# Attention with a routed feed-forward block: a builder's clock that lets loads overlap, and earlier ranks for V tiles 8 to 15

## The chip, the cores and the metric

The kernel runs on one core of one Trainium2 chip. The metric is the device time of one execution in microseconds (us). The core's engines are TensorE (PE, with its weight loads shown apart as PEld), VectorE (DVE), ScalarE (ACT) and GpSimd (POOL); SyncE (SP) issues nearly all DMAs.

## The reference

```python
B, S, D = 8, 3136, 256;  d_qk = 64;  F = 1024;  cap = 128
scores = (z @ z.T) / S                       # per batch, S x S, symmetric
attn = np.maximum(scores, 0.0) ** 2
x = u * (attn @ v)                           # S x D
s = x @ w_gate                               # per batch: one score per row
top = the 128 rows with the largest s
out = x;  out[top] = x[top] + sigmoid(s[top]) * (relu(x[top] @ w1) @ w2)
```

Everything is float32. Nearly all of the work is `z @ z.T` and `attn @ v` for 8 batches of 3136 rows; the routed part touches 128 rows per batch.

## The kernel before, in words

**Tiles.** A batch's 3136 rows are cut into six chunks of 512 queries and a remainder of 64 (`CHUNKS`), and into 24 tiles of 128 keys and a half tile of 64. Two neighbouring key tiles make a pair; a slot is one chunk of queries against one pair of key tiles. A slot's squared scores times V are added up in PSUM (`acc`, one for each half of the 256 columns, in two rotating accumulators), with V as the weights and the squares as the moving data, so the result stands transposed.

**Splitting.** PE multiplies rounded float32 (`F32R`). To keep the precision every operand is split in a rounded part and its remainder: `ZH` and `ZL`, the two halves of a `V` tile, and `hi` and `lo` of a slot's squares. A slot takes 16 matmuls with `hi` (both parts of V) and 8 with `lo` (rounded V alone), each over half of the rows of PE. A rounded part is made by ACT (a CAST or an ACTIVATE); a remainder is one subtraction of two operands in SBUF, on POOL or DVE, whichever the builder expects to end first. `lent` is a `hi` and `lo` pair that stands in a tile of the ring that otherwise holds `qk`.

**Symmetry.** The squares are symmetric, so a chunk computes only blocks with keys from its own chunk on. New blocks are made on PE (`sc`), lifted by ACT (`a`), squared, split, and also transposed on DVE (`aT`) and stored to DRAM (`squares`, `squares_own` for half of the diagonal block, `squares_last` for the remainder's keys). Later chunks fetch them as `qk`, `own` and `rest`; `rest_hl` holds both parts of a remainder block. A batch ends with its last chunk, made mostly of old blocks, with the 64 remainder rows among them, while the next batch's Z and V are already loaded and split; the next batch's first chunk is made of new blocks alone.

**V.** `stage_v` loads four V tiles (512 rows) with four DMAs into a tile `vst` of a ring of two, and `prep_v` rounds them pair by pair. The last use of a pair of the old batch frees its place for the new batch. In the first chunk of a batch the pairs are used in the order 0, 2 to 9, half tile, 10, 1, 11, and they are loaded and rounded in groups of two pairs in this order of first use.

**The order.** No order is written by hand. The Python builder keeps a clock for each engine and for the DMA queue (`Clock`, with constants for each kind of operation) and emits all engines' instructions in one program. Each waiting piece of work off PE is a job with a rank; among the jobs that can start, the one that starts first on that clock goes first, and the lower rank when they tie. PE is filled with whatever the clock says is ready. So the clock's times and the ranks set the order on every engine, and each engine then runs its own stream in that order on the chip. Ranks are counted in slots: a job of rank k belongs to slot k.

**What the change touches.** `Clock.move` (line 147) is the clock's account of a DMA: `begin` is when it may start, and `free(out)` is when earlier readers and writers of the part of the tile that it writes have ended. `free` has a second argument, `by`: entries of that engine are then left out. `prep_v` (line 759) sets the rank of the rounding of V and of its remainder, and the loop at lines 2653 to 2657 sets the rank of the loads of V; `k0` is the first slot of the batch and `first_use` the first slot that uses a pair. `fetch_rest` (line 860) issues two DMAs into one tile, whose columns alternate between the two.

Of the kernel before, what the change touches and what calls it, by code (L numbers as in the profile page):

```python
# [90 lines left out]
class Clock:  # L91
# [55 lines left out]
    def move(self, out, src, by):  # L147
        n = run = 1
        for _, c in out.ap:
            n *= c  # L150
        for s, c in sorted(src.ap, key=lambda x: x[0]):
            if s == run:
                run *= c
        short = 1
        for s, c in sorted(out.ap, key=lambda x: x[0]):
            if s == short:
                short *= c
        run = min(run, short, n)
        far, near = (x.space == bass.MemoryType.DRAM for x in (out, src))
        known = {(True, False): self.STORES.get(n), (False, True): self.LOADS.get(n), (False, False): self.INSIDE}.get((far, near))  # L160
        large = near and n > P * 2 * CH
        wait, took, more = known or (3.17 if large else 1.4, (1.25 if large else 1.0) * n / run * (0.008 + 0.000038 * 4 * run) / 16, 0.8)
        begin = max(self.at[by], self.after(src) + 0.06, 0.0 if far else self.free(out) + 0.06)
        self.at[by] = begin + (0.6 if far or out.ap[0][1] == 64 else 0.47 if out.ap[0][1] <= Q else 0.53)
        self.queue = max(self.queue, begin + wait, 2.4) + took
        return self.queue + more
# [179 lines left out]
def attention_then_routed_ffn(ctx: ExitStack, tc: tile.TileContext, zt, ut, v, wg, w1, w2, cst, cst16, keys, outs, at, cap):  # L346
# [43 lines left out]
    v_ring = Ring(stage, [P, GT, D], "vst", 2)  # L390
# [45 lines left out]
    def job(on, rank, fn, reads=(), rings=(), ok=None, took=None, locks=False):  # L436
        on = on.split("|")
        ready = reads if callable(reads) else max((clock.after(x) for x in reads), default=0.0) + 0.05
        j = Job(on, rank, fn, ready, rings, ok, took, locks)
        for e in on:  # L440
            pending[e].append(j)
# [81 lines left out]
    def more_steps(chain, steps):  # L523
        chain.steps.extend(steps)
        wake(chain)
# [6 lines left out]
    def round_on(e, hi, src):  # L532
        (nc.scalar.copy if e == "act" else ON[e].tensor_copy)(hi, src)

    def rest_on(e, lo, src, hi):
        ON[e].tensor_tensor(lo, src, hi.bitcast(F32), op=ALU.subtract)

    def takes(n):
        return {"pool": 0.15 + 0.00219 * n, "dve": 0.16 + 0.00104 * n + SPARE, "act": 0.19 + 0.00083 * n}
# [103 lines left out]
    for e in range(2):  # L643
        for f in range(0, NF // 2, 2):
            g = e * NF // 2 + f
# [25 lines left out]
    def stage_z(b, i, n=None, step=None, uses=1, queues=None):  # L671
        a, w = part(i)
        n = n or w
        if n > CH:
            st = old_ring.take("zall", uses=uses).rearrange("p f k -> p (f k)")
        else:
            st = z_ring.take("zst", uses=uses)
        for h in range(2):
            (queues or (nc.sync, nc.sync))[h].dma_start(st[h * 64 : h * 64 + 64, : step or n], zt[b, :, a : a + (step or n)])
        staged["z", b, i] = st  # L680

    def more_z(b, i, of):

        a, n = part(i)
        o = a - part(of)[0]
        for h in range(2):
            nc.sync.dma_start(staged["z", b, of][h * 64 : h * 64 + 64, o : o + n], zt[b, :, a : a + n])
# [49 lines left out]
    def z_free(b, i):  # L737
        return issued > max(last_key[b - 1, i], last_moving[b - 1, i])

    def stage_v(b, g, queues=None):  # L740

        whole = g < NJ // GT
        st = v_ring.take("vst", uses=2 if whole else 1)
        if whole:
            for f in range(GT):
                src = v[b, g * CH + f * P : g * CH + (f + 1) * P, :].rearrange("(t a) d -> a t d", a=Q)
                (queues or [nc.sync] * GT)[f].dma_start(st[f * Q : (f + 1) * Q], src)
        else:
            for h in range(2):
                nc.sync.dma_start(st[h * 64 : h * 64 + 64, 0, :], v[b, NJ * P :, :])  # L750
        staged["v", b, g] = st
        for i in range(2 if whole else 1):
            prep_v(b, 2 * g + i)
# [5 lines left out]
    def prep_v(b, g):  # L759

        st = staged["v", b, g // 2]
        src = st[:, g % 2 * 2 :]
        n = 2 if 2 * g < NJ else 1
        ring = pair_ring if n == 2 else half_ring
        src = src[:, :n].rearrange("p a d -> p (a d)").rearrange("p (f h i) -> p h f i", h=NK, i=Q)
        rank = first_use[b, g] + (-0.5 if b or g > 1 else 0.5)
        order = b * (NJ // 2 + 1) + sum((first_use[b, i // 2 * 2], i) < (first_use[b, g // 2 * 2], g) for i in range(NJ // 2 + 1))

        def high(e):
            t = ring.take("V", F32R)  # L770
            vtile[b, g] = t
            parts_of = [t[:, w].rearrange("p h (f i) -> p h f i", i=Q) for w in range(2)]
            round_on(e, parts_of[0], src)
            vnext[0] = order + 1
            for q in range(n):
                V[b, 2 * g + q] = t[:, :, :, q * P : (q + 1) * P]
            job("pool|dve", rank, lambda e: low(e, parts_of), [src, parts_of[0]], took=takes(n * D))

        def low(e, parts_of):
            rest_on(e, parts_of[1], src, parts_of[0])  # L780
            for q in range(n):
                vlow[b, 2 * g + q] = True
            v_ring.drop(st)

        landed = clock.after(src) + (SLACK if b else 0.05)
        turn = lambda: vnext[0] == order and (order < 2 or now[0] > 0 or 0 in parts)
        job("act" if b else "act|dve" if g > 1 else "dve", rank, high, lambda: landed, [ring], turn, takes(n * D), True)
# [31 lines left out]
    begins, ends, last_key, first_use, last_use, last_moving = {}, {}, {}, {}, {}, {}  # L819
# [551 lines left out]
    def load_u(b, c):  # L1371
        c0, w = CHUNKS[c]
        t = u_ring.take("ut")
        nc.sync.dma_start(t, ut[b, :, :, c0 : c0 + w].rearrange("h p t -> p h t"))
        chunk[b, c] = t
# [1256 lines left out]
    def at_slot(k, fn):  # L2632
        plan.setdefault(max(k, 0), []).append(fn)

    def load(k, rank, fn, rings=(), ok=None, reads=()):
        late = lambda: max([0.0] + [clock.after(x) for x in reads])
        at_slot(k, lambda: job("sp", rank, lambda e: fn(), late, rings, ok))

    for b in range(B):
        k0 = first_of[b, 0]  # L2640
        for c in range(NCH):
            if c < WHOLE:
                load(ends[b, c] - 9, ends[b, c] - 2, lambda b=b, c=c: load_u(b, c), (u_ring,))
        if b:

            def get_z(b=b, i=0):
                stage_z(b, i)
                prep_z(b, i, now[0] + 5)

            for i in range(NCH):  # L2650
                k = max(last_key[b - 1, i], last_moving[b - 1, i]) - LEAD + 1
                load(k, k0 - 12 + i, lambda b=b, i=i: get_z(b, i), (z_ring,), lambda b=b, i=i: z_free(b, i))
            for g in range(0, NJ // 2 + 1, 2):
                k = last_use[b - 1, g]
                before = [x for x in range(0, NJ // 2 + 1, 2) if first_use[b, x] < first_use[b, g]]
                ok = lambda k=k, b=b, before=before: now[0] >= k - 2 and all(("v", b, x // 2) in staged for x in before)
                load(max(k - 4, k0 - 16), k0 - 14 if g < 4 else first_use[b, g] - 4, lambda b=b, g=g: stage_v(b, g // 2), (v_ring,), ok)
        elif b == 0:
            load(0, 1, lambda: (more_z(0, 4, 1), prep_z(0, 4, 2, 1)))
            load(1, 2, lambda: (stage_z(0, FIFTH, S + 64 - FIFTH * CH, uses=2), prep_z(0, FIFTH, 4, FIFTH), prep_z(0, WHOLE, 5, FIFTH)), (old_ring,))  # L2660
            for g in range(4, NJ // 2 + 1, 2):
                k = first_use[0, g]
                load(max(0, k - 8), k - 4, lambda g=g: stage_v(0, g // 2), (v_ring,))
        at_slot(first_of[b, 2], lambda b=b: more_steps(far, turn_rest_u(b)))

    order_of = {}
    for k, (b, c, js, is_old) in enumerate(slots):
        key = b, c, js[0] // GT
        if is_old and c < WHOLE and key not in order_of:
            n = order_of[key] = len(order_of)  # L2670
            ok = lambda key=key, n=n: fetches[0] == n and stored.get((key[0], key[2], key[1])) == 2
# [6 lines left out]
        elif is_old and c == WHOLE:  # L2678
            g = js[0] // GT
            ok = lambda b=b, g=g: all(stored.get((b, g + i, WHOLE)) == 2 for i in range(2))  # L2680
# [37 lines left out]
    far = chain_of([], 3)  # L2718
# [171 lines left out]
```

## Time and profile before

| | us |
|---|---|
| median of 3 runs | 2033.03 (2032.85, 2033.03, 2036.61) |
| the profiled execution's own time | 2036.05 |
| its span, first to last instruction | 2034.2 |
| PE busy | 2000.0 (98%) |
| DVE, ACT, POOL busy | 1538.1, 1482.4, 1557.7 (76%, 73%, 77%) |
| DMA | 408.49 MB, mean 201 GB/s |

Busy time is counted from the records of instructions; PE runs two matmuls at a time, one on each half of its rows, and their ends are modelled, so the idle time between them is more telling than the busy share. The granted clock is 0.999 of full speed over the span. All program rows carry line 248, that of the recording helper, so rows are told apart by the names of their tiles. In the timeline a bracket at a row's end gives the time in which the engine stood idle before it, and what ended it.

### The profile page before, as it was taken

The numbers are of one execution on the slowest core, as the hardware profiler recorded it, in microseconds if no ns is written. First come the engines' busy times: TensorE is split into PE (matmuls) and PEld (weight loads), VectorE is DVE, ScalarE is ACT, GpSimd is POOL, SyncE is SP. The second block draws the span as 40 slices with busy tenths as digits, with TensorE's granted clock in tenths as the row PEclk, the third lists the DMA queues.
The fourth block names the chain that finished last, engine by engine and source line by source line (L and its number), as shares of the span: only waits on it lengthen the run. The fifth ranks groups of instructions, "written<-read, shape, count | busy, mean of one in ns | idle before, by whom it ended". The sixth has DMA issues, their size and how long they took to land. (4 is left out here: it accounts for less than half of the span.)

```text
span 2034.2 us, 45720 instructions
## 1 busy us (share of the span) xinstructions
PE 2000.0 (98%) x17226; PEld 1642.6 (81%) x17226; DVE 1538.1 (76%) x2563; ACT 1482.4 (73%) x1816; POOL 1557.7 (77%) x1096
## 2 busy tenths in 40 slices
PE   9999999999999999999999999999999999999998
PEld 6999878888787788888877788877887888877776
DVE  7776777667887758767789766887677676797786
ACT  8886788767887658776787657886678776887652
POOL 7787887779877778678977777867697777888662
PEclk9999999999999999999999999999999999999999
DMA  6899867886688767878767787778877868766862
GB/s 191 238 250 247 210 188 213 205 199 170 198 236 194 199 191 223 221 194 193 183 208 199 192 209 202 218 199 217 214 180 228 218 175 205 194 186 184 219 170 75
DMA packets 421614, 408.49 MB, mean 201 GB/s; under 512 B 128910, under 2 KB 329232, under 8 KB 421392
## 3 DMA queue, kind: packets, MB, share of 16 engines
q1 hardware_dynamic: 420224, 403.07, 74.3%
q8 instruction: 135, 2.21, 0.5%
q0 software_dynamic: 800, 2.10, 0.3%
q14 instruction: 87, 0.71, 0.1%
q10 hardware_dynamic: 368, 0.39, 0.1%
HBM read 230.08 MB, written 175.37 MB: 199 GB/s over the span
## 5 line engine op out<-in xcount | busy, mean ns | idle before, releaser
L248 PE MATMUL acc<-hi,V 64*128 64x512 f32 x8752 | 1153.9, 390 | 3.7 <-DVE sum L248 2.5
L248 PEld LDWEIGHTS acc<-hi,V 64*128 64x128 f32 x8752 | 844.0, 185 | 159.1 <-DVE sum L248 4.7
L248 PE MATMUL acc<-lo,V 64*128 64x512 f32 x4232 | 619.9, 391 | 9.9 <-POOL lo L248 6.3
L248 POOL TENSOR_TENSOR lo<-a,hi 128x512 fp32r<-128x512 f32 x288 | 450.4, 1572 | 183.3 <-ACT a L248 108.1
L248 POOL TENSOR_TENSOR lo<-qk,hi 128x512 fp32r<-128x512 f32 x315 | 486.9, 1561 | 72.1 <-ACT hi L248 45.3
L248 PEld LDWEIGHTS acc<-lo,V 64*128 64x128 f32 x4232 | 409.7, 184 | 95.3 <-POOL lo L248 17.8
L248 ACT ACTIVATE hi<-a 128x1024 fp32r<-128x1024 f32 (+2 forms) x385 | 346.8, 901 | 99.2 <-PE acc L248 66.0
L248 DVE STREAM_TRANSPOSE aT<-a 128x512 f32<-128x512 f32 (+2 forms) x622 | 383.5, 646 | 36.4 <-ACT a L248 25.2
L248 ACT ACTIVATE a<-a 128x1024 f32<-128x1024 f32 (+1 forms) x351 | 332.3, 949 | 78.2 <-DVE a L248 65.3
L248 ACT ACTIVATE a<-sc 128x1024 f32<-128x1024 f32 (+2 forms) x344 | 325.0, 945 | 76.7 <-PE sc L248 39.6
L248 DVE TENSOR_TENSOR lo<-a,hi 128x512 fp32r<-128x512 f32 x243 | 262.7, 1085 | 148.2 <-ACT a L248 75.9
L248 ACT CAST hi<-qk 128x1024 fp32r<-128x1024 f32 x240 | 249.4, 1046 | 138.9 <-PE acc L248 73.4
L248 DVE TENSOR_TENSOR lo<-qk,hi 128x512 fp32r<-128x512 f32 x165 | 180.3, 1105 | 55.1 <-ACT hi L248 49.9
L248 POOL TENSOR_TENSOR lo<-own,hi 128x256 fp32r<-128x256 f32 x94 | 100.7, 1091 | 82.5 <-ACT hi L248 55.0
L248 PE MATMUL sc<-ZH 64*128 64x512 f32 (+2 forms) x728 | 153.9, 381 | 5.9 <-ACT a L248 4.2
L248 PE MATMUL sc<-ZL,ZH 64*128 64x512 f32 (+2 forms) x728 | 152.2, 376 | 0.0
L248 PE MATMUL acc<-lent,V 64*128 64x512 f32 x1128 | 141.0, 390 | 3.8 <-POOL V L248 2.3
L248 POOL TENSOR_TENSOR ut<-x,w_run 128x512 f32<-128x512 f32 x90 | 131.5, 1474 | 9.1 <-DVE x L248 8.0
L248 PE MATMUL sc<-ZH,ZL 64*128 64x512 f32 (+2 forms) x680 | 132.2, 371 | 0.0
L248 PEld LDWEIGHTS acc<-lent,V 64*128 64x128 f32 x1128 | 105.2, 184 | 29.5 <-POOL V L248 4.0
L248 POOL TENSOR_TENSOR ut<-sum,ut 128x512 f32<-128x512 f32 x68 | 93.6, 1377 | 40.3 <-DVE sum L248 30.5
L248 POOL TENSOR_TENSOR lent<-a,lent 128x512 fp32r<-128x512 f32 x64 | 90.8, 1431 | 26.6 <-DVE a L248 14.1
(233 smaller groups left out, 1823.7 us busy)
## 6 DMA issues: line engine op xcount, KB each, us to landing
squares<-aT SPq DMA_DIRECT2D x240, 512.0 KB, 4.4
qk<-squares SPq DMA_DIRECT2D x480, 256.0 KB, 6.2
ut<-in_ut SPq DMA_DIRECT2D x48, 512.0 KB, 7.9
vst<-in_v SPq DMA_DIRECT2D x190, 128.0 KB, 3.2
out<-x SPq DMA_DIRECT2D x188, 128.0 KB, 4.2
squares_own<-aT SPq DMA_DIRECT2D x47, 256.0 KB, 2.0
own<-squares_own SPq DMA_DIRECT2D x188, 64.0 KB, 2.9
zst<-in_zt SPq DMA_DIRECT2D x85, 128.0 KB, 5.3
```

The lines of the kernel that those rows point to most:

```text
L248: got = real(*args, **kw)
```

## The change

The builder's clock no longer lets a DMA wait for earlier DMAs of the same queue into the same part of a tile, or out of it. From the second batch on, the rounding of V pairs 4 to 7 (tiles 8 to 15) and its remainder get a rank 4.5 slots ahead of their first use instead of 0.5, and these tiles are loaded with the rank of the first eight (14 slots ahead of the batch) instead of 4 slots ahead of their first use.

```diff
@@ Clock.move
-        begin = max(self.at[by], self.after(src) + 0.06, 0.0 if far else self.free(out) + 0.06)
+        begin = max(self.at[by], self.after(src) + 0.06, 0.0 if far else self.free(out, by) + 0.06)
@@ prep_v
-        rank = first_use[b, g] + (-0.5 if b or g > 1 else 0.5)
+        rank = first_use[b, g] - (4.5 if b and 4 <= g < 8 else 0.5 if b or g > 1 else -0.5)
@@ the loads of V, for b > 0
-                load(max(k - 4, k0 - 16), k0 - 14 if g < 4 else first_use[b, g] - 4, lambda b=b, g=g: stage_v(b, g // 2), (v_ring,), ok)
+                load(max(k - 4, k0 - 16), k0 - 14 if g < 8 else first_use[b, g] - 4, lambda b=b, g=g: stage_v(b, g // 2), (v_ring,), ok)
```

The three lines emit no instruction of their own; they change which piece of work the builder takes next. The kinds of instructions and their counts stay, but for the slots whose `hi` and `lo` stand in a lent tile (47 before, 44 now), and for remainders that go to POOL or to DVE. The order is the same on every engine up to some 245 us into the program and differs from there to nearly the end.

On PE, at the end of the first batch: `sc` rows are scores of the next batch, `hi`, `lo` products of the last old slots. Before:

```order
L248 MATMUL acc<-hi,V 128x512 x12
L248 MATMUL acc<-lo,V 128x512 x8
L248 MATMUL sc<-ZH 128x512 x2
L248 MATMUL sc<-ZH,ZL 128x512 x2
L248 MATMUL sc<-ZL,ZH 128x512 x2
L248 MATMUL acc<-hi,V 128x512 x14
L248 MATMUL acc<-lo,V 128x512 x2
L248 MATMUL acc<-hi,V 128x512 x2
L248 MATMUL acc<-lo,V 128x512 x2
L248 MATMUL acc<-hi,V 128x512 x8
L248 MATMUL acc<-lo,V 128x512 x6
```

The same place on PE now:

```order
L248 MATMUL acc<-hi,V 128x512 x16
L248 MATMUL acc<-lo,V 128x512 x8
L248 MATMUL acc<-hi,V 128x512 x8
L248 MATMUL sc<-ZH 128x512 x2
L248 MATMUL sc<-ZH,ZL 128x512 x2
L248 MATMUL sc<-ZL,ZH 128x512 x2
L248 MATMUL acc<-lo,V 128x512 x4
L248 MATMUL acc<-hi,V 128x512 x8
L248 MATMUL acc<-lo,V 128x512 x4
L248 MATMUL acc<-hi,V 128x512 x8
L248 MATMUL acc<-lo,V 128x512 x4
```

The last two old slots ran as 14, 2, 2, 2, 8 and 6 matmuls and now run as alternating groups of 8 `hi` and 4 `lo`. The old sequence stands at five of the seven batch ends, the new one at four, and a fifth is close to it.

On POOL, at the same place: `V` rows are remainders of V tiles of the next batch, `lo<-qk,hi` those of old slots, `ZL` and `ZH` those of the next batch's Z. Before:

```order
L248 TENSOR_TENSOR V<-vst,V 128x512 x2
L248 TENSOR_TENSOR lo<-qk,hi 128x512 x2
L248 TENSOR_TENSOR rest_hl<-rest,rest_hl 128x8x64
L248 TENSOR_TENSOR lent<-a,lent 128x512
L248 TENSOR_TENSOR ZL<-zst,ZH 128x4x4x32
L248 TENSOR_TENSOR lent<-a,lent 128x512
L248 TENSOR_TENSOR lo<-qk,hi 128x512 x3
L248 TENSOR_TENSOR V<-vst,V 128x512 x2
```

The same place on POOL now:

```order
L248 TENSOR_TENSOR V<-vst,V 128x512 x2
L248 TENSOR_TENSOR lo<-qk,hi 128x512 x2
L248 TENSOR_TENSOR ZL<-zst,ZH 128x128
L248 TENSOR_TENSOR ZH<-zst,ZH 128x64
L248 TENSOR_TENSOR lo<-qk,hi 128x512 x2
L248 TENSOR_TENSOR V<-vst,V 128x512 x2
L248 TENSOR_TENSOR lent<-a,lent 128x512
L248 TENSOR_TENSOR ut<-sum,ut 128x512
```

Between the first two V pairs and the next two POOL had five `lo<-qk` rows, three of them at the end, and two `lent`; now it has four `lo<-qk` and no `lent`.

On SP, from the first chunk of the second batch: `vst` rows are loads of V (four to a group of four tiles, `64x256` the half tile), the other loads and stores are as named above. Before:

```order
L248 DMA squares_own_0_120<-aT 128x512
L248 DMA zst<-in_zt 64x128 x2
L248 DMA out<-xr 64x256
L248 DMA vst<-in_v 32x4x256 x4
L248 DMA squares_0_97<-aT 512x1x256 x2
L248 DMA vst<-in_v 64x256 x2
L248 DMA squares_0_97<-aT 512x1x256
L248 DMA qk<-squares_0_97 32x4x512 x4
L248 DMA out<-x 32x16x64 x4
L248 DMA squares_0_97<-aT 512x1x256 x2
L248 DMA own<-squares_own_0_120 32x4x128 x4
L248 DMA vst<-in_v 32x4x256 x4
```

The same place on SP now:

```order
L248 DMA zst<-in_zt 64x128 x2
L248 DMA vst<-in_v 32x4x256 x12
L248 DMA squares_own_0_120<-aT 128x512
L248 DMA out<-xr 64x256
L248 DMA vst<-in_v 64x256 x2
L248 DMA squares_0_97<-aT 512x1x256 x3
L248 DMA qk<-squares_0_97 32x4x512 x4
L248 DMA out<-x 32x16x64 x4
L248 DMA squares_0_97<-aT 512x1x256
L248 DMA vst<-in_v 32x4x256 x4
L248 DMA squares_0_97<-aT 512x1x256
L248 DMA own<-squares_own_0_120 32x4x128 x4
```

Tiles 16 to 19 are now loaded in one row of twelve DMAs with tiles 8 to 15, ahead of the store of `squares_own`, and the last load of V (tiles 20 to 23) has moved ahead of the `own` fetch.

## Rows read from the trace of the kernel before

**Rows 1.** The page's first part: busy us (share) xinstructions.

```profile
PE 2000.0 (98%) x17226; PEld 1642.6 (81%) x17226; DVE 1538.1 (76%) x2563; ACT 1482.4 (73%) x1816; POOL 1557.7 (77%) x1096
```

**Rows 2.** Busy time by stretch: stretch, its us, busy us (xinstructions) by engine.

```profile
250.00:300.00 50.00, 47.90 (x411) 37.77 (x410) 39.52 (x58) 41.34 (x53) 42.52 (x31) 1.00 0.62 183
490.00:545.00 55.00, 51.82 (x446) 41.31 (x445) 44.81 (x85) 45.13 (x58) 47.34 (x35) 1.00 0.60 178
740.00:985.00 245.00, 244.98 (x2150) 203.16 (x2148) 183.19 (x230) 188.07 (x229) 190.22 (x132) 1.00 0.77 202
985.00:1040.00 55.00, 52.17 (x450) 41.39 (x448) 45.46 (x85) 45.51 (x58) 47.02 (x35) 1.00 0.60 179
1040.00:1120.00 80.00, 75.55 (x666) 61.15 (x664) 74.50 (x151) 60.57 (x69) 58.56 (x44) 1.00 0.72 201
...
1500.00:1545.00 45.00, 43.97 (x375) 34.53 (x373) 39.06 (x55) 37.39 (x49) 40.62 (x30) 1.00 0.64 184
1740.00:1800.00 60.00, 58.44 (x505) 46.03 (x503) 52.75 (x112) 51.40 (x64) 53.12 (x39) 1.00 0.54 162
1985.00:2034.20 49.20, 39.47 (x285) 31.56 (x281) 32.60 (x122) 10.69 (x23) 11.07 (x10) 1.00 0.20 67
```

**Rows 3.** PE's waits from 250 to 2000 us: total us, times, longest us.

```profile
PE acc L248 <- POOL lo L248: 6.3, 9, 1.0
PE sc L248 <- ACT a L248: 2.6, 2, 1.3
PE acc L248 <- POOL V L248: 2.3, 4, 0.9
PE acc L248 <- DVE lo L248: 2.0, 1, 2.0
PE acc L248 <- DVE sum L248: 1.9, 6, 0.5
```

**Rows 4.** PE in order of time: start us, us, row [idle before, releaser].

```profile
254.16 0.50 PE L248 MATMUL acc<-lo,V 64*128 64x512 f32 x2 [0.95 <-POOL lo L248]
...
292.24 0.74 PE L248 MATMUL acc<-lent,V 64*128 64x512 f32 x4 [0.90 <-POOL V L248]
...
1743.49 0.50 PE L248 MATMUL acc<-lo,V 64*128 64x512 f32 x2 [0.95 <-POOL lo L248]
```

**Rows 5.** DVE and POOL in order of time, at two routing steps.

```profile
597.24 0.90 DVE L248 TENSOR_TENSOR lo<-a,hi 128x512 fp32r<-128x512 f32 x1
...
1092.54 7.14 DVE L248 TENSOR_TENSOR lo<-a,hi 128x512 fp32r<-128x512 f32 x1
...
1091.56 2.62 POOL L248 TENSOR_TENSOR ut<-x,w_run 128x512 f32<-128x512 f32 x2
...
1096.61 2.52 POOL L248 TENSOR_TENSOR lo<-qk,hi 128x512 fp32r<-128x512 f32 x2
```

**Rows 6.** SP's DMA issues in order of time, 230 to 290 us.

```profile
232.94 1.18 SPq L248 DMA_DIRECT2D rest<-squares_last  x2
...
240.29 7.86 SPq L248 DMA_DIRECT2D vst<-in_v  x8
248.52 0.34 SPq L248 DMA_DIRECT2D squares_own<-aT  x1
...
280.41 2.88 SPq L248 DMA_DIRECT2D own<-squares_own  x4
283.46 1.74 SPq L248 DMA_DIRECT2D vst<-in_v  x4
```

**Rows 7.** POOL and ACT in order of time at the first boundary.

```profile
251.39 5.38 POOL L248 TENSOR_TENSOR lo<-qk,hi 128x512 fp32r<-128x512 f32 x3
...
256.81 1.06 ACT L248 ACTIVATE lent<-a 128x1024 fp32r<-128x1024 f32 x1 [3.00 <-POOL lo L248]
```

**Rows 8.** Groups of instructions by form: xcount | busy us, mean ns | idle before.

```profile
L248 POOL TENSOR_TENSOR V<-vst,V 128x512 fp32r<-128x512 f32 x63 | 89.5, 1428 | 2.7 <-ACT V L248 1.4 <-DVE V L248 1.0 <-DMA vst<-in_v 0.4
```

**Rows 9.** ACT in order of time, where PE waits for scores near 537 us.

```profile
536.76 1.02 ACT L248 ACTIVATE a<-sc 128x1024 f32<-128x1024 f32 x1 [2.12 <-POOL lo L248]
```

## The prediction

> **What bounds the kernel now.** I read the busy times first. The reader is to see that PE is busy 2000.0 of the 2034.2 us of the span [rows 1]. The change adds and removes no product, so PE's work stays and only its 34.2 us of idle time is in play. Second come the stretches of the span, to see where that idle time lies [rows 2]: span minus PE is 2.10, 3.18, 2.83, 1.03 and 1.56 us in the five stretches around 250, 490, 990, 1500 and 1745 us, 10.70 in all. These are five of the seven places where one batch ends and the next begins. The batch boundary near 745 us falls at the head of a stretch of 245 us in which PE is idle 0.02 us, so such a boundary can be crossed without a stop. The last 49.2 us have 9.73 us of idle time, and 1040 to 1120 us has 4.45. Third I asked what PE waits for behind 250 us [rows 3]: lower halves of attention squares from POOL (6.3 us in 9 waits), roundings of V from POOL (2.3 in 4), scores waiting for ACT's `a` (2.6 in 2), and sums that free an accumulator (1.9 in 6). Fourth, the order of time on PE puts them at the boundaries [rows 4]: at 254.16 us 0.95 for `lo`, at 292.24 us 0.90 for V, and at 1743.49 us again 0.95 for `lo`. The `lo` wait of about 0.95 us stands at four boundaries (254, 494, 990 and 1743 us; 3.8 us together).
>
> **The time that the sum starts from.** The profiled execution took 2036.05 us, 1.85 us around its span. The median of the other runs is 2033.03, and the three are 2032.85, 2033.03 and 2036.61: two levels some 3.3 us apart, and the profile is on the upper one. The trace shows what may part them: one DVE subtraction at 1092.54 us took 7.14 us, where the same step of the routing, two batches earlier, took 0.90 [rows 5], and PE waited 2.0 us for it [rows 3]. I take 3.0 us off for that (2036.05 to 2033.03) and predict an execution without it.
>
> **The builder's clock (line 163).** `fetch_rest` issues two DMAs into interleaved columns of one tile. The old clock starts the second only when the first has ended, by its own constants 2.7 us later; in the trace SP issues such a pair in 1.18 us [rows 6]. So the plan was too late about these tiles and is now nearer to what the queue does. The clock issues nothing, it only moves choices, and PE's order is unchanged to its row 390, some 245 us in. From there the first eight V DMAs of the next batch stand behind a `qk` load and a Z load instead of ahead of them, `rest_hl` is multiplied whole before `hi`, and the last old slots of the batch run as regular groups of `hi` 8 and `lo` 4. In the old order PE reaches `lo` two matmuls at a time, which is what a starved engine looks like in an order.
>
> **The `lo` wait.** Before, POOL does three `lo` from 251.39 to 256.77 us, in a row, and ACT stands 3.00 us behind them before it can write the next `lent` tile [rows 7]. In the old order the last two ACT casts that feed these halves stand back to back, after nine other ACT rows; in the new one the first of the two comes before that, with four rows between them, and POOL does the halves in pairs with V and Z work between. I expect all four waits to go: -3.8 us. Bounds: -3.8, or nothing if the new last pair is as late. The five sums behind them (about 1.5 of the 1.9 us) I leave standing, since ACT still copies the accumulator just after a `lent` write.
>
> **The V waits.** They are not for tiles 8 to 15 themselves but for tiles 20 to 23, loaded last: only two staging tiles exist, so what is rounded earlier frees staging earlier. Before, the four DMAs of the last load are issued at 283.46 us, behind an `own` fetch of 2.88 us [rows 6]. In the new order they stand ahead of that fetch and of one store, so some 2.9 us earlier if SP comes to this place at the same time, against a wait of 0.90 at most. All four go: -2.3 us; bounds -2.3 and 0.
>
> **What V displaces.** The new rank places four V remainders of a batch ahead of `lo` work of slots up to four later. One costs POOL 1.43 us [rows 8]; the work is the same, only earlier. The scores' wait near 537 us follows from such a crowding: ACT stood 2.12 us behind a POOL `lo` [rows 9], which had begun behind a V remainder. Two such waits, 2.6 us; still two late V remainders stand near there, so I take half: -1.3, bounds -2.6 and 0 (and more than 0 in a rival below).
>
> **Added waits on SP.** After the boundary SP's order now has twelve V DMAs in a row where it had eight. With two staging tiles the last four wait for a rounding, and behind them on SP stand the store of `squares_own`, one of `xr` and then stores of `squares`. In the old order the eight already took 7.86 us with their waits, the store went out at 248.52 and was first read at 280.41 us [rows 6], so 32 us hide a delay of some microseconds. Cost nothing; if that cover were gone, it would be half of such a block more, some 4 us, at each boundary.
>
> **What else moves.** From row 391 on everything shifts, also far from V. Three fewer of the first chunk's tiles are kept in a lent tile, and seven `rest_hl` and seven Z remainders go from POOL to DVE, whose count of two-input operations stays about the same (511 and now 515 in the orders). New stops elsewhere lie between 0 (the stretch with 0.02) and 4.45 (the worst stretch without a starved boundary) [rows 2]; a gain there is possible too, but 9.3 us of the idle time outside the named stretches lies mostly before 250 us, where nothing moves. I take +1.5, nearer to the long quiet stretch. The end, from the last batch's own remainder on, has the same sequence in both orders (106 rows on PE), so its 9.73 us stay.
>
> **Sum.** 2036.05 - 3.0 - 3.8 - 2.3 - 1.3 + 1.5 = 2027.1 us, that is 5.9 below the median shown.
>
> **Rivals.** (B) *The wait only changes its owner.* At the boundary the next chunk needs an accumulator as well, and ACT's copy comes after the `lent` write that itself waits for the last `lo`. For it: sum waits, up to 0.5 us, are there already [rows 3]. Against it: the boundary near 745 us shows neither. Then only the V waits go: 2033.03 - 2.3 = 2030.7.
> (C) *V ahead of `lo` starves PE.* The remainders of tiles 8 to 15, put 4.5 slots ahead, land on POOL before the `lo` that PE needs next. Price: one of 1.43 us at each of five boundaries, 7.2 us, with none of the gains: 2040.2, slower. It decides from 4.1/7.2, more than half a remainder per boundary before the last `lo`. For it: ACT's and PE's waits behind POOL today. Against it: in the new order two `lo` pairs stand ahead of the second V pair, where three `lo` stood behind two V.
> (D) *Collisions of POOL and DVE.* In the 7.14 us case POOL ran six operations from 1091.56 to 1099.13 us without a pause, and DVE ended right after them [rows 5]. If the new order meets this twice in every execution, 2 x 3.0 us eat the gain: 2027.1 + 6.0 = 2033.1. The Trainium skill says in "SBUF — State Buffer" (Who interferes with whom) that a DVE operation with two SBUF inputs and a GpSimd operation exclude each other for a whole instruction, and that whichever was issued first decides. By that rule alone a DVE step would lose one POOL operation, some 1.3 us, and the case would cost nothing that can be measured; the trace shows a loss over six in a row, so the rule bears out the collision but not its size.
>
> **How the numbers follow.** The runs of this kernel agree within some 0.2% (4.1 us), so less than that can't be told from no change: below 2029.0 is faster, above 2037.1 slower. My forecast has 0.56 (0.53 of it faster, 0.03 within), B 0.18 (within), C 0.12 (slower), D 0.14 (0.11 within, 0.03 slower). That makes 0.53, 0.32 and 0.15. The range begins where all five starved stretches lose all their idle time, 2033.0 - 10.7 = 2022.3, rounded down to 2022, and ends between D and C at 2038.5, which leaves out most of C and a little below.
>
> **What would show it.** Right: no wait of 0.9 us for `lo` near 254, 494, 990 and 1743 us, none for V near 292, 531, 1027 and 1541 us, the last V load issued before the `own` fetch, idle time of the five stretches together under 5 us, the last 49 us as before. Wrong: PE waiting for POOL's `lo` longer than 0.95 us right behind a V remainder (C), sum waits grown to about 1 us (B), DVE operations of over 5 us with POOL unbroken beside them (D), or PE waiting for `rest_hl`, which would say that the clock is now too early about these loads.

## The result and the profile after

The changed kernel takes 2045.26 us (2043.74 to 2048.86), the kernel before 2032.94 on the same chip; the ratio is 1.0052 [1.0039, 1.0065]. One of its six executions took 3305.94 us at a granted clock of 0.556, and the range and the ratio leave it out (the median counts it). It is slower by half a per cent where 5.9 us less were forecast. The profiled execution took 2045.7 us, its span is 2043.8.

The page's first part of the changed kernel answers [rows 1]:

```profile
PE 2004.2 (98%) x17226; PEld 1635.5 (80%) x17226; DVE 1553.6 (76%) x2573; ACT 1483.8 (73%) x1810; POOL 1549.6 (76%) x1092
```

Span minus PE is 39.6 us where it was 34.2, and the same 17226 matmuls take 4.2 us more. These are the 9.6 us between the spans, and both parts need a cause. What PE waits for from 250 us on answers [rows 3] (in total us, times, longest us):

```profile
PE sc L248 <- ACT a L248: 10.6, 6, 3.4
PE acc L248 <- DVE sum L248: 3.3, 5, 1.5
PE acc L248 <- DVE lo L248: 3.2, 2, 2.8
...
PE acc L248 <- POOL lo L248: 0.9, 2, 0.7
```

The waits for POOL's `lo` went from 6.3 to 0.9 us, and those for POOL's V (2.3) have no row any more: what the prediction took out is out. A wait that was 2.6 us is now 10.6: scores that wait until ScalarE has read the scores before them (`a<-sc`). The order of time on PE shows where, beside [rows 4]; each gap is followed by the next group of `hi` products:

```profile
249.49 0.56 PE L248 MATMUL sc<-ZH 64*128 64x512 f32 x2 [3.07 <-ACT a L248]
...
250.70 3.17 PE L248 MATMUL acc<-hi,V 64*128 64x512 f32 x16
```

```profile
490.81 0.50 PE L248 MATMUL sc<-ZH 64*128 64x512 f32 x2 [1.07 <-ACT a L248]
...
491.62 1.55 PE L248 MATMUL acc<-hi,V 64*128 64x512 f32 x12
```

```profile
1498.58 0.50 PE L248 MATMUL sc<-ZH 64*128 64x512 f32 x2 [2.22 <-ACT a L248]
...
1499.62 2.77 PE L248 MATMUL acc<-hi,V 64*128 64x512 f32 x12
```

```profile
1741.39 0.80 PE L248 MATMUL sc<-ZH 64*128 64x512 f32 x2 [3.37 <-ACT a L248]
...
1742.83 2.48 PE L248 MATMUL acc<-hi,V 64*128 64x512 f32 x12
```

Four gaps, 9.73 us, all at boundaries between batches. Behind the gap of 1.07 us twelve `hi` products take 1.55 us, behind those of 2.22 and 3.37 us they take 2.77 and 2.48. The busy times of short stretches behind three of the gaps show why; the third number from the end is the granted clock:

```profile
249.50:253.00 3.50, 3.50 (x18) 2.83 (x20) 3.40 (x6) 3.43 (x6) 1.92 (x3) 0.54 0.26 71
...
490.80:494.30 3.50, 3.49 (x30) 2.90 (x32) 2.41 (x4) 3.42 (x6) 1.65 (x3) 1.00 0.18 57
...
1741.40:1744.90 3.50, 3.50 (x16) 2.85 (x18) 2.01 (x4) 3.43 (x6) 1.25 (x2) 0.51 0.21 69
```

After the long gaps TensorE runs at its lower level, 1.2 GHz, nearly through the stretch, and does 18 or 16 matmuls where it does 30 at 2.4 GHz. That costs (1 - 0.51) x 3.5 = 1.7 us more per gap. It happens after 249, 1498 and 1741 us, and after a gap of 2.84 us at 1162.77 that has another cause (see the port event below): four times 1.7 us, more than enough for the 4.2 us of extra busy time. The Trainium skill ("TensorE: Matmul & The Clock Gate", What's actually happening) says that the clock has two levels and is set by how busy the engine has been; the stretches agree.

What ScalarE does at the first of these places, in order of time:

```profile
245.41 1.05 ACT L248 CAST hi<-qk 128x1024 fp32r<-128x1024 f32 x1 [0.76 <-DMA qk<-squares]
248.27 0.24 ACT L248 CAST ZH<-zst 128x64 fp32r<-128x64 f32 x1 [1.82 <-DMA zst<-in_zt]
248.43 1.02 ACT L248 ACTIVATE a<-sc 128x1024 f32<-128x1024 f32 x1
249.52 1.06 ACT L248 ACTIVATE lent<-a 128x1024 fp32r<-128x1024 f32 x1
```

A rounding of 0.24 us, the upper half of Z's half piece for the next batch, stands ahead of `a<-sc`. Its data isn't there, ScalarE takes its work in order, and so `a<-sc` starts late and PE with it. At 489.59, 1495.30 and 1740.17 us the same rounding stands 1.25, 3.10 and 1.66 us (in the last case behind 2.06 us at a late fetch of squares). In all ScalarE stands 28.4 us at 16 Z roundings between 228 and 2010 us, and 15.6 at V; before, no Z rounding waits for a load, and those of V wait 2.6 us. Part of this standing costs PE nothing: 2.18 us at 737.70 and 2.83 at 1238.02, at two other boundaries, leave no gap on PE. The load is issued here, on SP:

```profile
239.53 0.43 SPq L248 DMA_DIRECT2D ut<-in_ut  x1
240.06 1.15 SPq L248 DMA_DIRECT2D zst<-in_zt  x2
245.30 13.23 SPq L248 DMA_DIRECT2D vst<-in_v  x12
258.63 0.38 SPq L248 DMA_DIRECT2D squares_own<-aT  x1
```

It now follows a load of 512 KB. Before, on SP and on ScalarE:

```profile
249.28 1.12 SPq L248 DMA_DIRECT2D zst<-in_zt  x2
```

```profile
257.96 0.59 ACT L248 COPY sum<-acc 128x512 f32<-128x512 f32 x1
258.44 0.25 ACT L248 CAST ZH<-zst 128x64 fp32r<-128x64 f32 x1
```

How long a DMA takes to land is in the rows of issues (xcount, KB each, median us from issue to landing); the changed kernel, and then the kernel before, where the same load is issued behind a store of 256 KB, with the eight V loads before it already issued:

```profile
zst<-in_zt SPq DMA_DIRECT2D x2, 32.0 KB, 7.7
```

```profile
zst<-in_zt SPq DMA_DIRECT2D x2, 32.0 KB, 2.3
```

Over all seven batches with such a load the medians are 7.5 and 2.6 us. So the chain is: the new clock thinks SP's loads done earlier; the builder places this load 9 us earlier, where it lands 7.7 us after its issue, and its rounding earlier still than the landing; ScalarE stands; PE stands; the clock drops. In the order of ScalarE the rounding stood behind a copy of `sum` before, and now ahead of `a<-sc`. That the rounding's place makes the gap is tested by the first experiment.

### The profile page after: what moved, and what is told of

It is laid out like the page before. It is cut to its first block, busy times and chain, and to the rows that moved or that the text cites. A ratio compares the mean times of both kernels' runs of the same rounds, so it can differ in the third digit from the quotient of the medians.

```text
span 2043.8 us, 45693 instructions
## 1 busy us (share of the span) xinstructions
PE 2004.2 (98%) x17226; PEld 1635.5 (80%) x17226; DVE 1553.6 (76%) x2573; ACT 1483.8 (73%) x1810; POOL 1549.6 (76%) x1092
## 5 line engine op out<-in xcount | busy, mean ns | idle before, releaser
L248 POOL TENSOR_TENSOR lo<-a,hi 128x512 fp32r<-128x512 f32 x309 | 474.8, 1546 | 195.1 <-ACT a L248 103.4
L248 POOL TENSOR_TENSOR lo<-qk,hi 128x512 fp32r<-128x512 f32 x310 | 477.2, 1552 | 90.5 <-ACT hi L248 61.0
L248 ACT ACTIVATE hi<-a 128x1024 fp32r<-128x1024 f32 (+2 forms) x388 | 351.3, 906 | 101.9 <-PE acc L248 66.7
L248 POOL TENSOR_TENSOR lo<-own,hi 128x256 fp32r<-128x256 f32 x87 | 90.6, 1060 | 68.5 <-ACT hi L248 42.0
L248 PE MATMUL acc<-lent,V 64*128 64x512 f32 x1056 | 131.8, 388 | 0.2
L248 POOL TENSOR_TENSOR ut<-sum,ut 128x512 f32<-128x512 f32 x70 | 98.2, 1404 | 38.7 <-DVE sum L248 30.7
L248 POOL TENSOR_TENSOR V<-vst,V 128x512 fp32r<-128x512 f32 (+1 forms) x70 | 100.3, 1440 | 23.0 <-ACT V L248 17.1
```

Source lines behind the costliest of these rows:

```text
L248: got = real(*args, **kw)
```

## The experiments

All were timed in five rounds beside the kernel before (2034.0 to 2034.8 us in these rounds, some 20 runs each). Theory Z is the chain above. "Slack" is what the builder adds to the landing it counts on before it places a rounding; it is 2 us.

**The same plan, the rounding moved back.** The Z half is rounded when its remainder is due; the clock is told the old place, so nothing else moves.

```diff
-                round_on(e, to[0], src[:, :64])
+                if b: clock.note("act", "copy", [to[0]], [src[:, :64]])
+                else: round_on(e, to[0], src[:, :64])
...
             def low(e):
+                if b: tc.nc.scalar.copy(to[0], src[:, :64])
```

> The changed kernel with one instruction per batch moved: the CAST of the Z half (ZH<-zst 128x64) is issued on ACT when its remainder is issued, which puts it one or two rows later on ACT, behind the scores' lift (a<-sc) at four of the seven boundaries; the builder still counts it at the old place, so all other rows keep their order. Theory Z (ACT, which runs in order, stands at this cast for a Z load that lands late, and PE waits for the scores behind it): the waits for ACT a near 249, 490 and 1741 us (7.5 us together) and the stretches at half clock behind two of them go, the one near 1498 us stays, 2034 to 2038 us. Rival S (the loss is spread over the reordering, most of it in the last batch's routing): 2043 to 2046 us.

Measured: 2041.70 us (2035.26 to 2049.78), ratio 1.0033 [1.0021, 1.0046]. ScalarE at the first boundary (L733 is the moved rounding), and PE there and at 1491 us:

```profile
246.70 1.01 ACT L248 ACTIVATE a<-sc 128x1024 f32<-128x1024 f32 x1
248.28 0.25 ACT L733 CAST ZH<-zst 128x64 fp32r<-128x64 f32 x1 [0.56 <-DMA zst<-in_zt]
```

```profile
247.77 0.50 PE L248 MATMUL sc<-ZH 64*128 64x512 f32 x2 [0.22 <-ACT a L248]
...
248.58 2.00 PE L248 MATMUL acc<-hi,V 64*128 64x512 f32 x16
...
1491.69 0.50 PE L248 MATMUL sc<-ZH 64*128 64x512 f32 x2 [2.90 <-ACT a L248]
```

Where `a<-sc` came ahead of the rounding, the gap went from 3.07 to 0.22 us and sixteen `hi` products from 3.17 to 2.00; the gap at 490 us is down from 1.07 to 0.61, and the gap at 1741 is gone. At 1491.69 the rounding still stands ahead, and so does the gap. This is the cleanest of the runs for the mechanism, since no other instruction moved, and it is nearly what theory Z said of the gaps. Its size is less clean. The median gained 3.6 us only and lies between the ranges of theory Z and rival S, so neither had the time right. The profiled execution is the fastest of the twelve, 2035.26 us, 10.4 less than the changed kernel's; most of the others lie at 2040 to 2045, and no trace shows what those add. Nor are the 10.4 us all the rounding's. The gap of 2.84 us at 1162.77 and the lower clock behind it, some 4.5 us, are gone as well, because the DVE subtraction that PE waited for there ran long in one execution and short in the other. The changed kernel, and then this run:

```profile
1158.19 4.53 DVE L248 TENSOR_TENSOR lo<-a,hi 128x512 fp32r<-128x512 f32 x1 [1.56 <-ACT a L248]
```

```profile
1155.98 0.70 DVE L248 TENSOR_TENSOR lo<-a,hi 128x512 fp32r<-128x512 f32 x1 [1.56 <-ACT a L248]
```

The order on DVE and POOL is the same in both.

**One edit at a time.** The clock's line alone, the two rank edits, and each of them:

> The kernel before with the clock's line alone; the ranks of V are the old ones. Theory Z: in this order too the Z half is loaded early and its cast stands ahead of a<-sc on ACT, so PE waits for ACT a at the same boundaries, 2038 to 2046 us. Rival C (V remainders put ahead of lo starve PE): without the ranks there is no loss, 2030 to 2035 us.

> The kernel before with the ranks of V (rounding and load) alone; the clock is the old one. Theory Z: the cast of the Z half stays late, no waits for ACT a at the boundaries, 2029 to 2036 us. Rival C: the loss is here, 2038 us or more, with PE waiting for POOL lo right behind V remainders.

> The rounding edit alone: V tiles 8 to 15 are rounded with a rank 4 slots smaller, while the clock and the loading are those of before. Theory L: 2030 to 2038, no `hi` wait over 1.5 us at a boundary, since the loads still come when they came. Rival R: 2044 to 2058, with the `hi` waits of the run with both rank edits.

> The loading edit alone: V tiles 8 to 15 of a batch are due at first_use k0 - 14 as in the changed kernel, while the clock and the rounding rank are those of before. Theory L (SP takes its DMAs in order; a V load due early stands on SP for a V buffer of the old batch, 5.9 us from 235.46 to 241.31 in the run with both rank edits, and the square fetch behind it comes at 247.07 where it came at 235.74 before, so ScalarE's rounding of it is late): 2044 to 2058, with four or five waits of TensorE for ScalarE's `hi` of 2.5 to 3.4 us at 256, 500, 1002, 1515 and 1758 us. Rival R (the V roundings stand ahead of the `hi` roundings on ScalarE because of their own smaller rank): 2031 to 2037 here, with no wait for `hi` over 1.5 us.

| edit alone | us | ratio |
|---|---|---|
| clock's line | 2047.84 | 1.0070 [1.0050, 1.0091] |
| both rank edits | 2056.22 | 1.0117 [1.0099, 1.0134] |
| rounding rank | 2047.02 | 1.0052 [1.0032, 1.0073] |
| loading rank | 2059.02 | 1.0112 [1.0098, 1.0127] |

Every part loses alone; the two with the loading edit lose clearly more than the whole (1.0052 [1.0039, 1.0065]). With the clock's line alone ScalarE stands at the same loads (ScalarE's waits), so theory Z held in its mechanism; the time is 2 us above its range:

```profile
ACT ZH L248 <- DMA zst<-in_zt: 21.5, 15, 2.9
...
ACT V L248 <- DMA vst<-in_v: 16.7, 13, 2.2
```

For the two rank edits its expectation (2029 to 2036) was wrong. Rival C had the sign and the size, but not the place: PE's largest wait is not for POOL's `lo` (2.3 us in all) but for ScalarE's `hi` (16.3 us). SP's issues and PE with the loading edit alone:

```profile
232.97 1.18 SPq L248 DMA_DIRECT2D rest<-squares_last  x2
239.46 4.45 SPq L248 DMA_DIRECT2D vst<-in_v  x8
243.95 1.15 SPq L248 DMA_DIRECT2D zst<-in_zt  x2
245.14 2.02 SPq L248 DMA_DIRECT2D qk<-squares  x4
```

```profile
254.16 2.12 PE L248 MATMUL acc<-hi,V 64*128 64x512 f32 x16 [2.94 <-ACT hi L248]
```

Eight V loads stand ahead of the fetch of squares; SP stands from 234.15 to 239.46 us until staging is free, and the squares are asked for at 245.14 where it was 235.74. ScalarE rounds them at 253.06, as soon as they land, and PE has waited 2.94 us; such waits come to 15.7 us in seven places. That is theory L's chain, 1 us above its range; rival R fell with this run (2059 where it gave 2031 to 2037). The rounding edit alone was a miss for theory L (2030 to 2038 expected). Its trace, of an execution of 2041.76 us, shows the same form on DVE, not the `hi` waits that R asked for. DVE, then PE:

```profile
1275.88 1.30 DVE L248 STREAM_TRANSPOSE x<-ut 128x512 f32<-128x512 f32 x2 [2.62 <-DMA out<-xr]
1277.10 1.86 DVE L248 STREAM_TRANSPOSE aT<-a 128x512 f32<-128x512 f32 x3
```

```profile
1278.96 0.50 PE L248 MATMUL sc<-ZH 64*128 64x512 f32 x1 [2.48 <-ACT a L248]
```

By the view DVE stands 2.62 us until a store has landed, behind it come transposes that ScalarE needs to be done, behind those the scores. This is one such gap (another of 1.65 us at 780); the rest of its 13 us isn't settled.

**The V loads behind the squares.** The loading edit alone, but due 6 slots ahead of the batch and not 14.

```diff
-... k0 - 14 if g < 8 else first_use[b, g] - 4 ...
+... k0 - 14 if g < 4 else k0 - 6 if g < 8 else first_use[b, g] - 4 ...
```

> The loading edit alone, but V tiles 8 to 15 due at k0 - 6 in place of k0 - 14: on SP the eight V loads then stand behind the Z piece and the second fetch of squares, not ahead of them (and still ahead of U's load). Theory L (it was the V loads standing on SP ahead of that fetch that cost 24 us): 2030 to 2041, no wait of TensorE for ScalarE's `hi` of over 1.5 us at the batches' boundaries, where the run with k0 - 14 had 2.6 to 3.3 us at five of them. Rival Q (early V loads cost by their traffic or their rounding, wherever they stand): 2050 to 2062.

Measured: 2036.20 us, ratio 1.0011 [1.0000, 1.0023]. SP's issues:

```profile
235.43 3.87 SPq L248 DMA_DIRECT2D qk<-squares  x4
239.55 6.28 SPq L248 DMA_DIRECT2D vst<-in_v  x8
245.88 0.43 SPq L248 DMA_DIRECT2D ut<-in_ut  x1
```

The same loads, issued at nearly the same time (239.55 and 239.46), but with the squares ahead of them: 23 us less, and no wait for ScalarE's `hi`. The four V loads after them also come later, at 258.86 in place of 249.22 us, so the run moves two groups of loads and not one. Theory L held, Q fell.

**More slack in the changed kernel.** First 6 us more for the Z half; then 4 us more for V too; then 2 us for V. The edit holds for every batch from the second on, where two of the expectations say batches 1 to 3.

```diff
-job("act", rank, high, lambda: clock.after(src) + (SLACK if b else 0.05), ...
+job("act", rank, high, lambda: clock.after(src) + (SLACK + 6.0 * (i == WHOLE) if b else 0.05), ...
-        landed = clock.after(src) + (SLACK if b else 0.05)
+        landed = clock.after(src) + (SLACK + 2.0 if b else 0.05)
```

> The changed kernel, replanned with the builder waiting 6 us longer after the load before it places the cast of the Z half (SLACK 8 instead of 2 for this piece, from the second batch on). Theory Z: no ACT a waits at the boundaries, and the lo waits of before stay away, 2027 to 2034 us. Rival S: 2040 us or more, since the rest of the reordering stays.

> The changed kernel, planned again with more slack between the landing that the builder counts on and the rounding on ScalarE: 6 us for the half Z piece and 4 us for every V piece of batches 1 to 3. Theory Z (what the change lost is ScalarE standing at loads that land later than the builder counts on; in the run with 6 us for the Z half alone the V loads were left, ScalarE standing 3.24 and 2.41 us at them at 741 and 1237 us and TensorE 2.47 and 2.18 us behind it): 2024 to 2031, ScalarE's waits for V under 6 us in all where they were 18.9, no wait of TensorE of 2 us or more between 230 and 2000 us. Rival S (later rounding makes TensorE wait for V or for the lower halves again, as before): 2033 to 2041, waits for POOL V or POOL lo of over 6 us in all.

> As the run with 6 us for the half Z piece and 4 us for V, but 2 us for V. Theory Z: between the run with no slack for V (2035.7) and that with 4 us, so 2026 to 2034, with ScalarE's waits for V between 6 and 14 us in all. Rival S: 2033 to 2041. Rival N (a plan's total is set by chance: any shift of the numbers by which the builder orders moves some 200 instructions and the total by several us either way, whatever ScalarE waits for): no order between the two, and a total that the waits for V don't follow.

Measured: 2035.69, ratio 1.0001 [0.9991, 1.0012]; 2033.28 (2026.23 to 2040.29), 0.9998 [0.9984, 1.0012]; 2029.37 (2026.58 to 2030.54), 0.9969 [0.9958, 0.9980]. The first and the second miss theory Z's ranges by 2 us, the third is in it. With slack for the Z half alone the waits for `a` fell from 10.6 to 3.6 us (1.50 and 1.27 are left at two boundaries), and the next load in line took the place. ScalarE, DVE and PE of that run:

```profile
740.99 1.14 ACT L248 CAST V<-vst 128x512 fp32r<-128x512 f32 x2 [3.24 <-DMA vst<-in_v]
742.15 0.64 ACT L248 COPY xr<-acc 64x256 f32<-64x256 f32 x2
```

```profile
742.16 1.35 DVE L248 TENSOR_TENSOR V<-vst,V 128x512 fp32r<-128x512 f32 x1 [3.69 <-ACT V L248]
743.44 1.39 DVE L248 TENSOR_TENSOR xr<-acc,xr 64x512 f32<-64x512 f32 x2
```

```profile
744.98 0.49 PE L248 MATMUL sc<-ZH 64*128 64x512 f32 x2 [2.47 <-DVE xr L248]
```

ScalarE stands 3.24 us at V, the copy that frees an accumulator comes behind it, DVE's part behind that, and PE loses 2.47 us (and 2.18 at 1241.54). With 2 us more for V as well these two waits are gone (1.31 us is left at 744.00), and the kernel is faster than before, by 0.3%. ScalarE still stands 11.0 us at Z and 5.9 at V. What PE waits for:

```profile
PE acc L248 <- POOL lo L248: 4.2, 6, 1.8
PE sc L248 <- ACT a L248: 2.6, 3, 1.3
```

With 4 us ScalarE stands even less at V (4.8 us against 5.9), and yet the time scatters from 2026 to 2040. The profiled one, 2031.43 us, has one gap of 3.33 us behind this DVE row:

```profile
1153.58 5.00 DVE L248 TENSOR_TENSOR lo<-a,hi 128x512 fp32r<-128x512 f32 x1 [1.56 <-ACT a L248]
```

POOL ran without a pause from 1153.09 to 1158.03 us. This missed the expectation that no wait of 2 us is left. So the totals don't follow ScalarE's waits alone, and part of rival N stands.

**Is the slack the gain?** The same slack in the kernel before, and with the clock's line alone.

> The kernel before, with the larger slack alone (6 us more for the half Z piece, 2 us more for V pieces of batches 1 to 3), clock and ranks as before. Theory Z (the slack mends what the change broke: before, ScalarE stood 0 us at Z and V loads, so there is nothing to mend): 2033 to 2041, no gain. Rival G (the slack is a gain of its own, and the 2029.4 of the changed kernel with slack owes nothing to the change): 2026 to 2031.

> The clock's line and the larger slack, no rank edit. Theory Z (the clock's line by itself lost 13 us, 2047.8 against 2034.6, because ScalarE stood 21.5 us at Z loads and 16.7 us at V loads that the builder now counts on too early): 2027 to 2037, ScalarE's waits for Z and V loads together under 20 us where they were 38.2. Rival N (every new plan scatters by several us whatever ScalarE waits for): a total over 2040 with those waits nearly gone, or under 2037 with the waits still at 30 us or more.

Measured: the kernel before with the slack takes 2050.53 us, ratio 1.0080 [1.0066, 1.0093]; with the clock's line and the slack 2030.43, ratio 0.9981 [0.9971, 0.9991]. So rival G fell: of these plans the slack pays only in those with the new clock, where it takes the 13 us loss of the clock's line back, with ScalarE's waits at

```profile
ACT ZH L248 <- DMA zst<-in_zt: 14.2, 12, 2.7
```

for Z and 5.4 us for V, 38.2 together with the clock's line alone. Beside the 2029.37 us with all three edits and the same slack the intervals overlap, so the two rank edits add nothing that can be told. But the 2050.53 also missed theory Z's 2033 to 2041. Its trace shows a row like those of [rows 5],

```profile
1505.56 8.42 DVE L248 TENSOR_TENSOR lo<-a,hi 128x512 fp32r<-128x512 f32 x1
```

with POOL busy without a pause from 1505.95 to 1513.43 us, PE waiting 3.57 us for it and a lower clock behind. That explains some 5 of 16 us; the rest is open. The old plan has no early Z rounding to mend, and a new plan can meet a collision.

**Without the loading edit.** The version of 2029.37, less the edit that loads V tiles 8 to 15 earlier.

> The changed kernel with the larger slack (2029.4), less the edit that loads V tiles 8 to 15 earlier. The prediction's step on V (the four waits for V at 292, 531, 1027 and 1541 us, 2.3 us in all, go because these tiles are loaded earlier): 2030 to 2034, with the waits for V back. Rival E (the waits for V go by the clock's line and the rounding's rank anyway): 2027 to 2031, no wait for V. Rival L2 (the early loads hold SP up in this plan too): under 2027.

Measured: 2027.42 us (2025.93 to 2029.93), ratio 0.9969 [0.9957, 0.9980], the fastest run here, and by its interval not to be told from the version with the edit. No wait for V came back, so rival E held.

## Why the prediction was wrong

**The step that failed** is the one on the builder's clock: "the plan was too late about these tiles and is now nearer to what the queue does", and "The clock issues nothing, it only moves choices". The first half was read from SP's issue times, 1.18 us for a pair. A rounding doesn't wait for the issue but for the landing, and there the plan became too early: 7.7 us from issue to landing for the Z half where it had been 2.3. The step priced the choices that it saw moving (`hi`, `lo`, V) and not what an in-order ScalarE does with a rounding placed ahead of its data: 9.73 us in four gaps, and three times 1.7 us of lower clock behind them, some 15 us in the profiled execution. The sum had no term for it. How much of it is in the median is not shown: moving the rounding alone gave 3.6 us back, the slack, which plans everything anew, 9.6 to 16. The order of SP ahead of the prediction shows the half Z load moved ahead of the V loads; the prediction did not ask which ScalarE row waits for it. The list of what would show it wrong has "the clock is now too early about these loads", but looks for it at `rest_hl`.

**The `lo` waits** (-3.8): right; all four are gone, and the row fell by 5.4 us.

**The V waits** (-2.3): right in size, wrong in cause. They stay away without the loading edit too, and they are gone with the clock's line alone and with the loading edit alone, and down to 0.2 us with the rounding edit alone. So the earlier loads can do it but are not needed, and why every one of these plans does it is not shown.

**The scores' waits** (-1.3): those near 537 and 1033 us are gone, as half expected, but the same row of waits grew to 10.6 us with other places.

**The port event** (-3.0): too large. Larger samples put the kernel before at 2034.0 to 2034.8 us, not at 2033.03, so 1.0 to 1.8 of the 3.0 were not there to take, and in the trace before PE lost 2.04 us to the event, at a granted clock of 1.00 behind it. The subtraction of 7.14 us is gone from 1092 us, and two others have come: 4.53 us at 1158.19, with POOL unbroken from 1157.20 to 1162.16 and PE waiting 2.84 us, and 5.03 us at 1384.49, with PE waiting 0.33. That is rival D's mechanism, twice in this trace (D's condition was twice in every execution), at very unequal prices; it adds to the loss and is not the main part of it.

**SP's waits** (nothing): right in this combination, where the squares are fetched at 237.53 us, ahead of the twelve V loads; SP stands with them for 13.23 us, and the store of `squares_own` at 258.63 us has cover enough. It is not right as a rule: the argument looked at the stores behind a standing SP, and with the loading edit alone it was a load behind it that cost 23 us.

**Stops elsewhere** (+1.5): too small. It was taken from a stretch that ran without a stop in the old plan, which says nothing of a new one: the collision at 1158.19 and the lower clock behind it alone make 4.5 us. The last 49 us stayed as forecast: from the last product with the own remainder to the end 45.4 us, before 45.0.

**The rivals.** B and C fell. Sums do wait longer, 1.46 us at 1796 and 1.21 at 1884, but not at the boundaries where B put them, and no wait for `lo` is over 0.7. C came out near in time for a reason that wasn't its own. With the clock's error covered by slack, the time is 2029.4 us or, without the loading edit, 2027.4, near the forecast of 2027.1. That is in part luck: the waits for `lo` are 4.2 and 2.8 us there, so 2.1 and 3.5 of the 3.8 went, the slack is a new plan as well, and in the kernel before it cost 16 us.

## What to carry to other kernels

When an edit makes a planner think that transfers end earlier, look in the order for each operation on an in-order engine that reads such a transfer, and ask what stands right behind it; what decides is the landing, counted from the issue in the place where it now stands, and not the issue time. A load that waits for a buffer is such an operation too: it holds up every load behind it on its queue. An edit that corrects one number of a planner can lose until its margins are set again, so try it with the margins moved, and time several plans: here one and the same slack took 16 us off one plan and put 16 us on another.

## What the runs showed of the hardware

- One and the same load of twice 32 KB landed 2.3 us after its issue where it followed a store of 256 KB, and 7.7 us behind a load of 512 KB on the same queue, which itself took 8.2 (median over the kernel 2.6 and 7.5).
- In the changed kernel gaps on TensorE of 2.22, 2.84, 3.07 and 3.37 us were each followed by a stretch at the lower clock that cost about 1.7 us; the gap of 1.07 us was not. In other runs gaps of 2.94 us (the loading edit alone, at 254.16) and 2.47 us (slack for the Z half, at 744.98) were followed by a granted clock of 1.00, and one of 1.93 us (the loading edit alone, at 791.63) by 0.61. So the length of a gap alone doesn't tell.
- A DVE subtraction of two tiles in SBUF took 4.5, 5.0, 7.1 and 8.4 us beside unbroken runs of four to six POOL operations, ending at or just after the last of them. The Trainium skill ("SBUF — State Buffer", Who interferes with whom) has the one that comes second blocked for a whole instruction of the other; these rows show it blocked for a whole run of them. That is rare: in the changed kernel's trace 143 subtractions that make `lo` on DVE began inside an unbroken POOL run with 3.5 us or more of it still to come, and all but two (4.53 and 5.03 us) took 1.84 us or less. The order doesn't decide it: in the same order of DVE and POOL one subtraction took 4.53 us in one execution and 0.70 in another.
